# Chunked attention, an MLP and a routed MLP on one core: the first stage in another order, with products of zeros on TensorE

## The chip, the cores and the metric

The kernel runs on one core of a Trainium2 chip. The metric is the device time of one launch in microseconds (us). The kernel before takes 530.31 us, the median of three runs (529.72 to 530.44).

## The reference

Three layers follow one another. Sizes: 4 batches, 8 heads, 768 positions, head width 32, state 16, so 3072 tokens of 256 numbers.

```
# 1: chunked linear attention, chunks of 32
cum = cumsum(log(clip(a)))                  # decay inside a chunk
y   = ((C B^T) * exp(cum_i - cum_j) * causal) x  +  (C state) * exp(cum_i)
state = exp(sum la) * state + sum_j B_j x_j exp(cum_end - cum_j)
# 2: gated MLP, 256 -> 1536 -> 256
x = (silu(x w_gate) * (x w_val)) w_out
# 3: routed MLP, 8 experts, the best one per token
h = relu(x w1[e]);  out = gate * (h w2[e])
```

## The kernel before

The work of layer 1 is cut into 24 *units* of 128 tokens; four units are a *block* of 512 tokens, the width of one product of layer 2. The first block has to be through layer 1 before the first product of layer 2 (line L441, tiles `pg` and `pv`) can start. This opening part, which `first_block` writes out by hand, is called the first stage here. Instructions of an engine run in the order in which the code issues them; an engine that waits holds up all that stands behind it. Loads go through one queue on SyncE (SP), also in order.

A unit u passes these steps, each a function:
- `load` (SP): tiles `xbb` and `cbd`, 128x512 fp32 each (262 kB). There are four buffers of each.
- `weigh` (GpSimd, once VectorE): tile `xw`, L278.
- `scores_mm` (TensorE): 16 products of 64 columns (L291) and 16 of 256 (L297) in two PSUM tiles `pc`. `pc` and one of the two `py` tiles share a ring of three buffers.
- `scores_m` and `states` (VectorE, some of it ScalarE): `mt` (L305) and the states `sv`, `se`, `st`.
- `values_mm` (TensorE, L343 and L353): tiles `py`.
- `values_out`: four VectorE products `y`, `z` (L369 to L372), then a ScalarE cast into `xt` (L374), the high part of the token block.
- `values_low` (VectorE, L380): the low part of `xt`.

The decay factors come once for every two blocks: `setup_ln`, `setup_decay` (`pw`, `W`) and `setup_cum` (`pe`, `er`); `cum_split` leaves `er` and `eh`. `emit_d(b)` makes a tile `du` (L259, GpSimd) out of `er` for block b, and `emit_u(b)` two products `pu` (L270) with copies `U` on ScalarE. `U` of block 0 is needed by `values_out` of units 0 to 3, `U` of block 1 by units 4 to 7.

The MLP weights lie packed in memory. `load_w(f)` brings column tile f of twelve (`wraw`, 786 kB, three buffers). `decode(f, part)` unpacks it: part 0 (ScalarE, `ha`, L403), part "t" (ScalarE, `wv`, L406), parts "b" and "c" (VectorE, `wv`, L412 and L416), part 2 (ScalarE, high half `wh`, L419) and part 3 (low half `wl`, L421, VectorE, or GpSimd for f = 0). The three buffers make `load_w(f + 3)` wait for part "c" of f.

`keep_busy(n)` issues n products that nobody reads (`pi`, L204). After the first stage a loop over i issues per step twelve products of layer 2 (`mlp1_mm`: six `pg`, six `pv`), a silu on ScalarE (`h`, L448), a product on VectorE (`h`, L449), and from i = 2 on six products `py` (L469), with one attention unit in most steps. `pg`, `pv` and the second `py` tile share a ring of three PSUM buffers: the second `pv` waits until L449 has read the first.

Of the kernel before, what the change touches and what calls it, by code (L numbers as in the profile page):

```python
# [9 lines left out]
F32 = mybir.dt.float32  # L10
F32R = mybir.dt.float32r
BF16 = mybir.dt.bfloat16
# [17 lines left out]
BLK = 512  # L30
# [87 lines left out]
def kernel(  # L118
# [5 lines left out]
    nc = tc.nc  # L124
# [64 lines left out]
    def setup_cum(b0, n):  # L189

        p = ps_g("pe", (128, n, 132))
        for b in range(n):
            nc.tensor.matmul(out=p[:, b], lhsT=at[:, 2 * (b0 + b):2 * (b0 + b) + 2].rearrange("k b t c -> k (b t c)"),
                             rhs=c1[:, C_S:C_S + 132], start=True, stop=True)
        nc.scalar.activation(out=er[:, b0:b0 + n], in_=p, func=AF.Exp, scale=-1.0)

    idle_t = []

    def keep_busy(n):

        if not idle_t:
            idle_t.append(ps.tile([128, 2, 256], F32, tag="y0", bufs=1, name="pi"))
        for _ in range(n):
            nc.tensor.matmul(out=idle_t[0], lhsT=r32[:, 0],  # L204
                             rhs=r32.rearrange("p g j -> p (g j)").unsqueeze(1).to_broadcast([128, 2, 256]),
                             start=True, stop=True)

    def silu_first():

        t = ap_.tile([128, 1], F32, name="sf")  # L210
        nc.scalar.activation(out=t, in_=c1[:, C_ME:C_ME + 1], func=AF.Silu)

    def setup_ones():
        p8 = c1[:, C_P8:C_P8 + 8].unsqueeze(2)
        nc.vector.tensor_copy(out=r16.rearrange("p (h n) -> p h n", h=8), in_=p8.to_broadcast([128, 8, 16]))
        nc.vector.tensor_copy(out=r32.rearrange("p g (h i) -> p (g h) i", h=4), in_=p8.to_broadcast([128, 8, 32]))
# [19 lines left out]
    def cum_ends(b0, n, d2):  # L236
        p = ps_g("pe2", (128, 8 * n, 4))
        nc.tensor.matmul(out=p.rearrange("p a b -> p (a b)"), lhsT=r16, rhs=d2.rearrange("p a b c -> p (a b c)"),
                         start=True, stop=True)
        return p  # L240
# [8 lines left out]
    def emit_d(b):  # L249
        if b == 1:  # L250
            d = keep.tile([128, 4, 128], F32R, name="du", tag="yT", bufs=1)
        else:
            d = ap_.tile([128, 4, 128], F32R, name="du", tag="mt", bufs=2)
        o = C_MU + 4 * (b % 2)
        if b == 2:
            for q in range(4):
                nc.scalar.activation(out=d[:, q], in_=er[:, b // 2, 0:128], func=AF.Copy, scale=c1[:, o + q:o + q + 1])
        else:
            nc.gpsimd.tensor_tensor(  # L259
                out=d, in0=er[:, b // 2, 0:128].unsqueeze(1).to_broadcast([128, 4, 128]),  # L260
                in1=c1[:, o:o + 4].unsqueeze(2).to_broadcast([128, 4, 128]), op=ALU.mult)
        return d
# [10 lines left out]
    def weigh(u, e):  # L273

        r = raw[u]
        b, o = divmod(u, 4)
        r["xw"] = ap_.tile([128, 8, 32], F32, name="xw", tag="xw", bufs=3)
        e.tensor_tensor(out=r["xw"], in0=r["x"], in1=W[:, b, o * 8:o * 8 + 8].unsqueeze(2).to_broadcast([128, 8, 32]),  # L278
                        op=ALU.mult)
# [107 lines left out]
    def load_w(f, e=nc.sync):  # L387
        if f >= NF:
            return
        wr[f] = keep.tile([128, 768, 2], I32, name="wraw", tag="raw", bufs=3)  # L390
        e.dma_start(out=wr[f], in_=I["mw"][f].bitcast(I32).rearrange("p (n t) -> p n t", t=2))
# [415 lines left out]
    def first_block():  # L807

        setup_loads()
        load(0)  # L810
        load(1)
        nc.sync.dma_start(out=at0[:, 2:], in_=I["at"][:, 2:])
        load(2)
        load_w(0)
        load(3)
        load_w(1)
        setup_ln(0, 2)
        setup_decay(0, 2)
        setup_cum(0, 1)
        weigh(0, nc.vector)  # L820
        scores_mm(0)
        cum_split(0, 1)
        setup_ones()
        weigh(1, nc.gpsimd)
        d = emit_d(0)
        p = cum_ends(0, 1, cum_ends_d(0, 1))
        scores_m(0)
        cum_store(0, 1, p)
        states(0)
        emit_u(0, d)  # L830
        cum_pairs(1, 8)
        setup_ln(2, NBLK)
        decode(0, 0)
        d = emit_d(1)
        weigh(2, nc.gpsimd)
        for u in range(4):
            scores_mm(u + 1)
            values_mm(u)
            if u == 1:
                setup_decay(2, NBLK)  # L840
                setup_cum(1, 2)
            if u < 3:
                scores_m(u + 1)
                states(u + 1)
            if u in (0, 2):
                decode(u // 2, "t")
            values_out(u)
            if u == 0:
                emit_u(1, d)
                decode(0, "b")  # L850
            if u == 1:
                decode(0, "c")
            if u == 2:
                decode(1, "b")
            keep_busy((0, 4, 4, 6)[u])
            values_low(u)
            load(u + 4)
            if u == 0:
                weigh(3, nc.gpsimd)
            if u == 1:  # L860
                load_w(2)
                load_w(3)
                nc.sync.dma_start(out=c2, in_=I["cst"][:, C1:C_END])
                weigh(4, nc.gpsimd)
                decode(0, 2)
                decode(0, 3, low=nc.gpsimd)
                decode(1, 0)
            if u == 2:
                decode(1, "c")
                silu_first()  # L870
                decode(1, 2)
                weigh(5, nc.gpsimd)
        scores_m(4)
        states(4)
        decode(1, 3)
        decode(2, 0, "t")
        load_w(4)

        todo = {0: 2, 1: 3, 2: 4, 4: 5, 6: 6, 8: 7, 10: 8, 12: 9, 14: 10, 15: 11}
        units = {0: 4, 1: 5, 3: 6, 5: 7, 13: 8, 16: 9, 19: 10, 22: 11}  # L880
        for i in range(2 * NF):
            q, f = divmod(i, HALF)
            b, f = q % 2, f + HALF * (q // 2)
            u = units.get(i)
            w = todo.get(i, NF)
            if i + 1 in units and units[i + 1] > 4:
                weigh(units[i + 1] + 1, nc.vector if i < 16 else nc.gpsimd)
            if u == 7:
                mlp1_down(*late.pop(0))
                scores_mm(u + 1)  # L890
                values_mm(u)
                values_out(u)
                values_low(u)
            p = mlp1_mm(b, 0, BLK, f)
            if u is not None and u != 7:
                scores_mm(u + 1)
                values_mm(u)
            if len(late) == LAG or u == 7:
                mlp1_down(*late.pop(0))
            late.append((b, 0, BLK, f))  # L900
            decode(w, 1)
            h = mlp1_h(p, BLK)
            if w < NF:
                load_w(w + 3)
                decode(w + 1, 0, "t")
            decode(w, 2)
            if u is not None and u != 7:
                values_out(u)
            decode(w, 3)
            if i in (20, 21):  # L910
                turn_y(0, 2 * i - 40)
                turn_y(0, 2 * i - 39)
            if i == 23:
                route_b(0)
            mlp1_split(h, b, 0, BLK, f)
            if i in (7, 13):
                take_part(0 if i == 7 else 1)
            if i == 19:
                take_y(0)
            if u is not None:  # L920
                if u != 7:
                    values_low(u)
                    scores_m(u + 1)
                    states(u + 1)
                load(u + 4)
            if i == 6:
                scores_m(8)
                cum_split(1, 2)
            if i == 7:
                dd.append(cum_ends_d(1, 2))  # L930
            if i == 8:
                cum_store(1, 2, cum_ends(1, 2, dd.pop()))
                cum_pairs(8, NU)
                states(8)
            if i == 9:
                dd.append(emit_d(2))
            if i == 10:
                emit_u(2, dd.pop())
            if 16 <= i < 20:
                setup_route(i - 16)  # L940
            if i == 22:
                route_a(0)
            if i == 21:
                dd.append(emit_d(3))
            if i == 23:
                emit_u(3, dd.pop())
# [190 lines left out]
```

## Time and profile before

| | us |
|---|---|
| median of three runs | 530.31 |
| profiled execution | 530.17 |
| its span | 528.4 |
| around the span | 1.77 |
| TensorE busy | 505.0 (96% of the span) |
| VectorE busy | 289.1 (55%) |
| first product of layer 2 begins at | 24.40 |

The span is what the profiler sees between the first and the last instruction. A time in the trace counts from the span's start. A row of the timeline gives start, duration, engine, line, operation, output and inputs, count, and in brackets the idle time of the engine before it and who ended it.

### The profile page before, as it was taken

How to read it: one execution, taken by the hardware profiler on the slowest of the kernel's cores; microseconds unless marked ns; L12 is line 12 of the kernel's file. 1: busy time of each engine (PE TensorE's matmuls, PEld its weight loads, DVE VectorE, ACT ScalarE, POOL GpSimd, SP SyncE). 2: the span in 40 equal slices, each digit the busy share in tenths (PEclk: the TensorE clock that was granted, in tenths of full speed). 3: DMA queues.
4: the chain of work that ended last, by engine and by line, in shares of the span. 5: the costliest groups of instructions: out<-in, count | busy, mean ns of one | idle time of the engine just before them, and what ended most of it. 6: DMA issues, size and time to landing. Idle time of an engine off the chain costs nothing.

```text
span 528.4 us, 11243 instructions
## 1 busy us (share of the span) xinstructions
PE 505.0 (96%) x4580; PEld 416.7 (79%) x4580; DVE 289.1 (55%) x631; ACT 219.5 (42%) x403; POOL 105.8 (20%) x127
## 2 busy tenths in 40 slices
PE   6889999999999999999999999999999999999990
PEld 3677787778788778888788778888899989999880
DVE  4998786944554544445444554455466564646320
ACT  4785575434333334233333332434454353534220
POOL 3200000220220130005000224211055426240220
PEclk9999999999999999999999999999999999999995
DMA  8954422011230312012100104234188544521100
GB/s 299 338 183 137 155 80 82 25 49 41 82 32 30 103 15 66 3 47 74 21 2 2 43 1 158 84 121 41 41 105 176 162 130 137 153 104 42 40 22 22
DMA packets 20694, 45.55 MB, mean 86 GB/s; under 512 B 4768, under 2 KB 8352, under 8 KB 20640
## 3 DMA queue, kind: packets, MB, share of 16 engines
q1 hardware_dynamic: 17424, 38.29, 26.2%
q0 software_dynamic: 3072, 6.41, 4.1%
q8 instruction: 37, 0.61, 0.6%
q14 instruction: 17, 0.14, 0.1%
q10 hardware_dynamic: 144, 0.11, 0.1%
HBM read 38.30 MB, written 6.50 MB: 85 GB/s over the span
## 4 chain that ended last, share of the span: by engine, by line
PE 76%; issue 11%; DVE 4%; POOL 3%; ACT 2%; DMA 1%; SPq 0%; POOLq 0%; DVEq 0%; ACTq 0%
PE py L469 19%; PE pg L441 18%; PE pv L441 18%; PE ph L758 7%; PE po L779 6%; PE pt L553 2%; POOL out L793 2%; PE pc L297 2%; PE py L353 1%; PE py L343 1%; PE pc L291 1%; DMA xbb<-in_xbb 1%; PE pu L270 1%; DVE wv L412 1%; PE px L747 1%
## 5 line engine op out<-in xcount | busy, mean ns | idle before, releaser
L441 PE MATMUL pg<-xt,wh 128*128 128x512 f32 x288 | 93.2, 404 | 0.3 <-ACT xt L374 0.2
L441 PE MATMUL pv<-xt,wh 128*128 128x512 f32 x288 | 90.4, 395 | 0.0
L449 DVE TENSOR_TENSOR h<-h,pv 128x512 f32<-128x512 f32 x72 | 49.4, 686 | 66.7 <-PE pv L441 55.6
L456 DVE TENSOR_TENSOR hl<-h,hh 128x512 fp32r<-128x512 f32 x72 | 50.2, 697 | 61.7 <-ACT hh L455 61.5
L758 PE MATMUL ph<-xt,hl 128*128 128x512 f32 x288 | 72.7, 394 | 0.0
L779 PE MATMUL po<-hl,hh 128*128 128x256 f32 x384 | 70.1, 283 | 0.0
L441 PEld LDWEIGHTS pv<-xt,wh 128*128 128x128 f32 x288 | 54.2, 188 | 12.8
L779 PEld LDWEIGHTS po<-hl,hh 128*128 128x128 f32 x384 | 60.3, 188 | 2.1
L455 ACT CAST hh<-h 128x512 fp32r<-128x512 f32 x72 | 44.6, 620 | 40.4 <-DVE h L449 40.4
L441 PEld LDWEIGHTS pg<-xt,wh 128*128 128x128 f32 x288 | 52.1, 188 | 11.6 <-ACT xt L374 0.6
L448 ACT ACTIVATE h<-pg 128x512 f32<-128x512 f32 x72 | 42.7, 593 | 41.7 <-PE pg L441 41.7
L614 POOL DMA_INDIRECT slots<-ids,si x24 | 26.0, 1081 | 168.4 <-DVE si L606 163.6
L758 PEld LDWEIGHTS ph<-xt,hl 128*128 128x128 f32 x288 | 51.7, 188 | 9.2
L469 PE MATMUL py<-hh,wh 128*128 128x512 f32 x144 | 58.7, 407 | 0.0
L441 PE MATMUL pg<-xt,wl 128*128 128x512 f32 x144 | 57.0, 396 | 0.3 <-DVE wl L421 0.3
L469 PE MATMUL py<-hl,wh 128*128 128x512 f32 x144 | 56.9, 395 | 0.0
L469 PE MATMUL py<-hh,wl 128*128 128x512 f32 x144 | 56.8, 394 | 0.0
L441 PE MATMUL pv<-xt,wl 128*128 128x512 f32 x144 | 56.8, 394 | 0.0
L779 PE MATMUL po<-hl,hl 128*128 128x256 f32 x192 | 53.9, 281 | 0.2 <-DVE hl L767 0.2
L767 DVE SCALAR_TENSOR_TENSOR hl<-ph,hh 128x512 fp32r<-128x512 f32 x48 | 33.0, 688 | 31.8 <-ACT hh L766 30.8
L766 ACT ACTIVATE hh<-ph 128x512 fp32r<-128x512 f32 x48 | 28.8, 600 | 41.4 <-PE ph L758 24.3
L779 PEld LDWEIGHTS po<-hl,hl 128*128 128x128 f32 x192 | 36.1, 188 | 0.4 <-DVE hl L767 0.4
(140 smaller groups left out, 669.6 us busy)
## 6 DMA issues: line engine op xcount, KB each, us to landing
eraw<-in_ew SPq DMA_DIRECT2D x24, 512.0 KB
wraw<-in_mw SPq DMA_DIRECT2D x12, 768.0 KB
xbb<-in_xbb SPq DMA_DIRECT2D x24, 256.0 KB
cbd<-in_cbd SPq DMA_DIRECT2D x24, 256.0 KB
yd<-yr SPq DMA_DIRECT2D x6, 528.0 KB
slots<-ids,si POOLq DMA_INDIRECT x24
xg<-yd,idx POOLq DMA_INDIRECT x24
out<-ob,idx POOLq DMA_INDIRECT x24
```

What stands on the lines that cost most here:

```text
L297: nc.tensor.matmul(out=r["pc"][g][32 * q:32 * q + 32, 0:256], lhsT=r["bt"][k, 32 * q:32 * q + 32], rhs=r["c"][k, q // 2].rearrange("p h i ...
L441: nc.tensor.matmul(out=t, lhsT=w[:, f, o:o + 128], rhs=xt[:, xp, k, cs], start=n == 0, stop=n == 5)
L448: nc.scalar.activation(out=h, in_=p[0], func=AF.Silu)
L449: nc.vector.tensor_tensor(out=h, in0=h, in1=p[1], op=ALU.mult)
L455: nc.scalar.copy(out=hh, in_=h)
L456: e.tensor_tensor(out=hl, in0=h, in1=hh.bitcast(F32), op=ALU.subtract)
L469: nc.tensor.matmul(out=yb[b][d][:, c:c + m], lhsT=w[:, f, o:o + 128], rhs=h, start=first and n == 0, stop=last and n == 2, skip_group_chec ...
L614: i = nc.gpsimd.indirect_dma_start(out=slots[0:E * upto], out_offset=bass.IndirectOffsetOnAxis(ap=si[:, s:s + 1], axis=0), in_=ids[g][:, o ...
L758: nc.tensor.matmul(out=p, lhsT=self.hl[:, w, o:o + 128], rhs=self.xt[:, xp, k], start=n == 0, stop=n == 5)
L766: nc.scalar.activation(out=hh, in_=p, func=AF.Relu)
L767: nc.vector.scalar_tensor_tensor(out=hl, in0=p, scalar=0.0, in1=hh.bitcast(F32), op0=ALU.max, op1=ALU.subtract)
L779: nc.tensor.matmul(out=self.po[s // 2][:, s % 2], lhsT=h[:, q], rhs=self.hl[:, w, o:o + DM], start=f == 0 and n == 0 and s % 2 == 0, stop= ...
```

## The change

The line numbers of the changed kernel are 12 to 15 higher behind its new function (L259 becomes L271, for example).

- `emit_d(0)` comes ahead of `weigh(1)`.
- A bf16 tile of zeros `zb` is set on VectorE, and nine products of 512 columns with it go to TensorE: five ahead of `setup_decay`, two ahead of `scores_mm(0)`, two behind `cum_ends`.
- `load_w(1)` moves behind `load(4)`, `load_w(2)` behind `load(6)`, `load_w(3)` behind `load(7)`.
- The decode of weight tile 0 moves one to two units later. That of tile 1 moves so that its parts "b", "c" and 2 stand behind unit 3's `values_low`.
- `emit_u(1)` moves from unit 0 to unit 2, `silu_first` (with its table load) from unit 2 to unit 3.
- `weigh(4)` and `weigh(5)` come ahead of the low half of tile 0 on GpSimd.
- `keep_busy` has 2, 2, 4, 4 products in place of 0, 4, 4, 6.

```diff
+    def warm_up(n):
+        if not warm_t:
+            warm_t.append(ap_.tile([128, BLK], BF16, name="zb"))
+            nc.vector.memset(warm_t[0], 0.0)
...
+            nc.tensor.matmul(out=idle_t[0].rearrange("p g j -> p (g j)"), lhsT=warm_t[0][:, 0:128], rhs=warm_t[0],
+                             start=True, stop=True)
...
-        load_w(1)
+        warm_up(5)
         setup_ln(0, 2)
         setup_decay(0, 2)
         setup_cum(0, 1)
+        warm_up(2)
         weigh(0, nc.vector)
         scores_mm(0)
         cum_split(0, 1)
         setup_ones()
+        d = emit_d(0)
         weigh(1, nc.gpsimd)
-        d = emit_d(0)
         p = cum_ends(0, 1, cum_ends_d(0, 1))
+        warm_up(2)
         scores_m(0)
...
-            if u in (0, 2):
-                decode(u // 2, "t")
+            if u == 2:
+                decode(1, 0)
             values_out(u)
...
+            if u == 3:
+                decode(1, "t")
+                silu_first()
...
         scores_m(4)
         states(4)
-        decode(1, 3)
+        decode(1, 1, 2, 3)
         decode(2, 0, "t")
         load_w(4)
```

GpSimd, from its first product on; `xw` is a unit's weighed input and `du` feeds `pu`. Before:

```order
L278 TENSOR_TENSOR xw<-xbb,W 128x256
L259 TENSOR_TENSOR du<-er,c_69 128x512 x2
L278 TENSOR_TENSOR xw<-xbb,W 128x256 x3
L421 TENSOR_TENSOR wl<-wv,wh 128x768
L278 TENSOR_TENSOR xw<-xbb,W 128x256
```

Now:

```order
L271 TENSOR_TENSOR du<-er,c_69 128x512
L290 TENSOR_TENSOR xw<-xbb,W 128x256
L271 TENSOR_TENSOR du<-er,c_69 128x512
L290 TENSOR_TENSOR xw<-xbb,W 128x256 x4
L433 TENSOR_TENSOR wl<-wv,wh 128x768
```

The first `du` no longer stands behind an `xw`, and the low half `wl` of weight tile 0 stands behind all five `xw`.

VectorE, at the end of the first stage: `mt`, `sv`, `se` are unit 4's, the `y`, `z` and `xt` rows unit 3's, and `wv` a weight tile in decode. Before, the `wv` rows are tile 1's, and so is `wl`:

```order
L412 SCALAR_TENSOR_TENSOR wv<-ha,wv 128x768
L380 TENSOR_TENSOR xt<-y_422,xt 128x2x128
L416 SCALAR_TENSOR_TENSOR wv<-wraw,wv 128x768
L369 TENSOR_TENSOR y_497<-py,U 128x192
L370 TENSOR_TENSOR z_498<-py,U 128x128
L371 TENSOR_TENSOR y_497<-py,U 128x64
L372 TENSOR_TENSOR y_497<-y_497,z_498 128x128
L380 TENSOR_TENSOR xt<-y_497,xt 128x2x128
L305 TENSOR_TENSOR mt<-pc,c_69 128x256 x2
L321 SCALAR_TENSOR_TENSOR sv<-se,eb,pc 128x64
L324 SCALAR_TENSOR_TENSOR se<-sv,eb,pc 128x64
L421 TENSOR_TENSOR wl<-wv,wh 128x768
```

Now (the first pair of `wv` is tile 1's, the second tile 2's):

```order
L384 TENSOR_TENSOR y_498<-y_498,z_499 128x128
L392 TENSOR_TENSOR xt<-y_498,xt 128x2x128
L317 TENSOR_TENSOR mt<-pc,c_69 128x256 x2
L333 SCALAR_TENSOR_TENSOR sv<-se,eb,pc 128x64
L336 SCALAR_TENSOR_TENSOR se<-sv,eb,pc 128x64
L424 SCALAR_TENSOR_TENSOR wv<-ha,wv 128x768
L428 SCALAR_TENSOR_TENSOR wv<-wraw,wv 128x768
L433 TENSOR_TENSOR wl<-wv,wh 128x768
L290 TENSOR_TENSOR xw<-xbb,W 128x256
L424 SCALAR_TENSOR_TENSOR wv<-ha,wv 128x768
L428 SCALAR_TENSOR_TENSOR wv<-wraw,wv 128x768
L461 TENSOR_TENSOR h<-h,pv 128x512
```

Tile 1's two `wv` steps have moved from ahead of unit 3's `xt` to behind unit 4's states, directly ahead of the `wl` that needs them.

ScalarE, from unit 3's cast into `xt` to the first silu `h`; `ha` and `wv` are the first steps of a decode, `wh` is its high half. Before:

```order
L419 CAST wh<-wv 128x768
L374 CAST xt<-y_497 128x2x128
L326 ACTIVATE st<-se,eb 128x64
L327 ACTIVATE st<-sv,eb 128x64
L403 ACTIVATE ha<-wraw 128x768
L406 ACTIVATE wv<-wraw 128x768
L448 ACTIVATE h<-pg 128x512
```

Now:

```order
L386 CAST xt<-y_498 128x2x128
L418 ACTIVATE wv<-wraw 128x768
L223 ACT_TABLE_LOAD
L223 ACTIVATE sf<-c_69 128x1
L338 ACTIVATE st<-se,eb 128x64
L339 ACTIVATE st<-sv,eb 128x64
L431 CAST wh<-wv 128x768
L415 ACTIVATE ha<-wraw 128x768
L418 ACTIVATE wv<-wraw 128x768
L460 ACTIVATE h<-pg 128x512
```

Tile 1's `wv`, the table load and tile 1's `wh` now stand between unit 3's cast and the first silu; the `ha` and second `wv` behind them are tile 2's, as before.

## Rows read from the trace of the kernel before

**Rows 1.** Windows: start and end, length, busy us by engine, PEclk, DMA share, GB/s

```profile
10.91:24.80 13.89, 11.93 (x351) 8.29 (x336) 12.28 (x37) 11.07 (x23) 3.70 (x4) 1.00 0.96 343
29.55:33.76 4.21, 2.76 (x13) 1.83 (x11) 4.08 (x12) 2.13 (x5) 0.00 (x0) 1.00 0.70 233
36.00:42.00 6.00, 6.00 (x28) 4.85 (x26) 5.88 (x15) 4.11 (x7) 0.00 (x0) 1.00 0.60 218
```

**Rows 2.** Timeline of TensorE: start, duration, instruction, idle time before it

```profile
3.41 0.69 PE L186 MATMUL pw<-at,c 128*128 128x64 f32 x2 [3.41 <-ACT at L182]
5.24 1.11 PE L297 MATMUL pc<-cbd,xbb 64*32 64x256 f32 x16
8.27 1.22 PE L270 MATMUL pu<-du,r 128*128 128x512 f32 x2 [1.60 <-POOL du L259]
15.90 0.27 PE L186 MATMUL pw<-at,c 128*128 128x128 f32 x1 [0.85 <-issue]
17.60 0.64 PE L297 MATMUL pc<-cbd,xbb 64*32 64x256 f32 x16
24.40 0.96 PE L441 MATMUL pg<-xt,wh 128*128 128x512 f32 x2 [0.21 <-ACT xt L374]
33.76 0.28 PE L291 MATMUL pc<-xw,xbb 64*32 64x64 f32 x7 [1.45 <-DVE mt L305]
```

**Rows 3.** Timeline of VectorE, from the split of the decay on

```profile
5.32 0.30 DVE L226 TENSOR_TENSOR er<-er,eh 128x132 f32<-128x132 f32 x1
7.64 0.22 DVE L316 TENSOR_TENSOR se<-st,pc 128x64 f32<-128x64 f32 x1
10.91 0.76 DVE L305 TENSOR_TENSOR mt<-pc,c 128x256 f32<-128x256 f32 x2 [2.46 <-PE pc L297]
13.47 0.96 DVE L412 SCALAR_TENSOR_TENSOR wv<-ha,wv 128x768 int32<-128x768 int32 x1 [0.65 <-ACT wv L406]
17.85 0.42 DVE L380 TENSOR_TENSOR xt<-y,xt 128x256 fp32r<-128x256 f32 x1 [0.25 <-ACT xt L374]
20.70 1.22 DVE L412 SCALAR_TENSOR_TENSOR wv<-ha,wv 128x768 int32<-128x768 int32 x1
22.17 0.94 DVE L416 SCALAR_TENSOR_TENSOR wv<-wraw,wv 128x768 int32<-128x768 int32 x1
24.38 0.42 DVE L380 TENSOR_TENSOR xt<-y,xt 128x256 fp32r<-128x256 f32 x1 [0.47 <-ACT xt L374]
25.89 0.95 DVE L421 TENSOR_TENSOR wl<-wv,wh 128x768 fp32r<-128x768 f32 x1
27.68 0.96 DVE L412 SCALAR_TENSOR_TENSOR wv<-ha,wv 128x768 int32<-128x768 int32 x1 [0.50 <-ACT wv L406]
29.55 0.68 DVE L449 TENSOR_TENSOR h<-h,pv 128x512 f32<-128x512 f32 x1
32.96 0.75 DVE L305 TENSOR_TENSOR mt<-pc,c 128x256 f32<-128x256 f32 x2
```

**Rows 4.** Timeline of GpSimd in the first stage

```profile
6.61 0.61 POOL L278 TENSOR_TENSOR xw<-xbb,W 128x256 f32<-128x256 f32 x1 [6.17 <-DMA xbb<-in_xbb]
7.18 2.17 POOL L259 TENSOR_TENSOR du<-er,c 128x512 fp32r<-128x512 f32 x2
12.01 0.62 POOL L278 TENSOR_TENSOR xw<-xbb,W 128x256 f32<-128x256 f32 x1 [2.09 <-DMA xbb<-in_xbb]
18.62 1.85 POOL L421 TENSOR_TENSOR wl<-wv,wh 128x768 fp32r<-128x768 f32 x1 [2.75 <-ACT wh L419]
```

**Rows 5.** Timeline of ScalarE: the first table load, a high half, two steps of a decode

```profile
1.16 1.28 ACT L176 ACT_TABLE_LOAD   x1 [1.16 <-PEq L1127]
23.15 0.83 ACT L419 CAST wh<-wv 128x768 fp32r<-128x768 f32 x1 [0.57 <-DVE wv L416]
25.95 0.90 ACT L403 ACTIVATE ha<-wraw 128x768 f32<-128x768 f32 x1
26.75 0.90 ACT L406 ACTIVATE wv<-wraw 128x768 int32<-128x768 uint32 x1
```

More of the change, by code (lines that the diff above doesn't have):

```diff
@@ L205, in keep_busy @@
                              rhs=r32.rearrange("p g j -> p (g j)").unsqueeze(1).to_broadcast([128, 2, 256]),
+                             start=True, stop=True)
+    warm_t = []
+    def warm_up(n):
+        if not warm_t:
+            warm_t.append(ap_.tile([128, BLK], BF16, name="zb"))
+            nc.vector.memset(warm_t[0], 0.0)
+            idle_t.append(ps.tile([128, 2, 256], F32, tag="y0", bufs=1, name="pi"))
+        for _ in range(n):
+            nc.tensor.matmul(out=idle_t[0].rearrange("p g j -> p (g j)"), lhsT=warm_t[0][:, 0:128], rhs=warm_t[0],
                              start=True, stop=True)
@@ L832, in first_block @@
         setup_ln(2, NBLK)
-        decode(0, 0)
         d = emit_d(1)
@@ L837, in first_block @@
             scores_mm(u + 1)
+            if u == 2:
+                emit_u(1, d)
             values_mm(u)
@@ L844, in first_block @@
                 states(u + 1)
-            if u in (0, 2):
-                decode(u // 2, "t")
+            if u == 2:
+                decode(1, 0)
             values_out(u)
             if u == 0:
-                emit_u(1, d)
+                decode(0, 0, "t")
+            if u == 1:
                 decode(0, "b")
-            if u == 1:
+            if u == 2:
                 decode(0, "c")
-            if u == 2:
-                decode(1, "b")
-            keep_busy((0, 4, 4, 6)[u])
+            if u == 3:
+                decode(1, "t")
+                silu_first()
+            keep_busy((2, 2, 4, 4)[u])
             values_low(u)
@@ L858, in first_block @@
             if u == 0:
+                load_w(1)
                 weigh(3, nc.gpsimd)
             if u == 1:
+                weigh(4, nc.gpsimd)
+            if u == 2:
                 load_w(2)
+                weigh(5, nc.gpsimd)
+                decode(0, 2)
+                decode(0, 3, low=nc.gpsimd)
+            if u == 3:
                 load_w(3)
                 nc.sync.dma_start(out=c2, in_=I["cst"][:, C1:C_END])
[L864 to L872, printed above, removed]
         scores_m(4)
         states(4)
-        decode(1, 3)
+        decode(1, 1, 2, 3)
         decode(2, 0, "t")
```

## The prediction

> **What bounds the kernel now.** I read the table of windows first, then the timeline engine by engine. Over the whole run TensorE is the bound, so the reader should look for the place from which it stays full. From 36 us on it is busy for 6.00 us of 6.00 [rows 1]. Its last long wait ends at 33.76: 1.45 us, released by VectorE's `mt` of unit 5, which ran at 32.96 [rows 2, 3]. So the end of the run moves as that `mt` moves, and later work behind it keeps its order.
>
> What sets that `mt` is VectorE. From 10.91, where `mt` of unit 1 starts, to 24.80, where unit 3's low part ends (24.38 and 0.42), VectorE is busy for 12.28 of 13.89 us; from the first `h` at 29.55 to 33.76 for 4.08 of 4.21 us [rows 1, 3]. TensorE's first product of layer 2 at 24.40 waits for the cast of unit 3 [rows 2], itself a link of this chain. Ahead of 10.91 VectorE had waited 2.46 us for unit 1's scores [rows 3]. These stood behind `pu`, which began at 8.27 after 1.60 us idle and waited for `du` on GpSimd [rows 2]; and `du` stood behind an `xw` that started at 6.61 because its input landed then [rows 4], though `er`, which `du` reads, was ready at 5.62 (5.32 and 0.30) [rows 3].
>
> [...]
>
> **The change, part by part.** I follow the VectorE chain: where it starts, how long it is, and what it hands to TensorE.
>
> *Start of the chain.* With `du` first on GpSimd it can run from 5.65 and, at 2.17/2 = 1.08 us [rows 4], be done at 6.75 in place of 8.27. Two other things then come late. One is the nine products of zeros. A `pu` takes 1.22/2 = 0.61 us at the lower level [rows 2], my upper bound; 0.35 us, that by the ratio 0.64/1.11, is the lower one; for the first ones I take 0.48, the middle. Nothing shows when the first could start; I take 1.2, about where ScalarE begins [rows 5]. Five then end at 1.2 + 2.4 = 3.6 (2.95 to 4.25), against 3.41 where `pw` started, so all that hangs on the decay comes 0.2 us late (0 to 0.85). The other four fill gaps: TensorE idled 1.60 us ahead of `pu`. The other late comer is a PSUM buffer: unit 1's scores need one that unit 0's `se` still reads, until 7.86 (7.64 and 0.22) [rows 3].
>
> The forecast takes it that the clock is at the upper level by then, since TensorE now has work from about 1.2 on with hardly a gap, where before it had its first long work at 8.27. Then `pu` is over before unit 0's states are, and unit 1's scores start at about 7.86 + 0.2 = 8.1. They take 0.64 us and a head of some 0.2 for the 64-column products: `mt` of unit 1 starts at 9.0, 1.9 us sooner.
>
> [...]
>
> *Length of the chain.* From 10.91 to the first `h` at 29.55 it was 18.64 us. Nothing is taken out of it: tile 1's two `wv` steps (20.70, 22.17) only move behind unit 3's low part and unit 4's states. What changes is the waits and one stretched instruction [rows 3, 5]:
> - The wait of 0.65 us ahead of tile 0's first `wv` (13.47) goes, since that step now comes one unit later. Unit 0's low part then has nothing between it and its cast, and waits as unit 3's does: 0.47. Together -0.18.
> - Tile 0's ScalarE steps now stand ahead of unit 1's cast, and they, with `W` and `er`, can hold its low part: 0 to 0.55, I take 0.30 in place of the 0.25 at 17.85: +0.05.
> - The 1.22 us of the `wv` at 20.70 should be like the 0.96 at 27.68: -0.26. This is a single stretched row; if it stretches again the term is nothing.
> - Tile 1's `wl` now stands directly behind its `wv`, with ScalarE's `wh` between: VectorE waits 0.83 + 0.05 = +0.88.
> - The old wait of 0.50 at 27.68 goes. In its place VectorE's next `wv` (tile 2) waits for ScalarE, which begins `ha` and `wv` only behind that `wh`: 26.75 - 25.95 + 0.90 = 1.70 us, against VectorE's own `wl` and `xw`, 27.68 - 25.89 - 0.50 = 1.29. So +0.41 - 0.50 = -0.09.
>
> Sum 18.64 - 0.18 + 0.05 - 0.26 + 0.88 - 0.09 = 19.04 us. The first `h` starts at 9.0 + 19.04 = 28.04, against 29.55: 1.51 us sooner. Unit 3's low part itself then ends at 28.04 less the stretch from it to `h`: 29.55 - 24.80 = 4.75, and 0.88 - 0.09, and the two `wv` at 29.55 - 27.68 = 1.87. That is 20.63, 4.17 sooner, of which 2.66 is given back ahead of `h`.
>
> *What that is worth.* From `h` to unit 5's `mt` the order of VectorE is as before, so TensorE's wait ends at 33.76 - 1.51 = 32.25 and the rest follows.
>
> *What is hidden.* The first product of layer 2 needs tile 0's `wl`, which GpSimd (1.85 us [rows 4]) now makes late in the stage. It may end about 1 us behind unit 3's cast, and delay the first twelve products by that. But TensorE then waits for ScalarE anyway: the second `pg` needs no PSUM buffer until the first is read by a silu that stands behind tile 2's steps, and the second `pv` waits for `h`. The first products move by about 4.1 us and `h` by 1.5, so this is worth nothing up to about 2.6 us, and beyond it each us costs one. The table load (1.28 [rows 5]) now lies after the last cast; ScalarE has that time, since its next due piece is `wh` behind the two `wv`. The 2 fewer `keep_busy` products stand in TensorE's idle time either way.
>
> *The loads.* They are in order and the DMA engines are full, 0.96 of the time at 343 GB/s [rows 1]. Unit 3's `xbb` lands at 12.01 [rows 4], with nothing changed ahead of it. Behind it come `cbd` 3, both tiles of unit 4, and only then weight tile 1: 3 x 0.262 + 0.786 = 1.57 MB, 4.6 us, so 16.6. Its first use on ScalarE, ahead of unit 2's cast, comes at about 17. This is close: 0.4 us of cover, and behind it each us costs VectorE one.
>
> *Sum.* 530.17 - 1.51 = 528.66 by the profiled execution, which is 0.14 below the median of the runs; so 528.8.
>
> **The rivals.**
> 1. *The clock rises later*, with the first `pu` or unit 1. For it: nothing in the trace shows TensorE on zeros, and before, its work from 3.41 on left it slow through the `pu` at 8.27. Against it: the far earlier start of the work. Then the four other zeros cost 4 x 0.48 less the 1.60 of idle time, and the 0.2 from the five: `pu` at 8.27 + 0.5 = 8.8; faster `pu` and scores give back 0.6 and 0.5, so `mt` starts near 10.6 - 0.4 = 10.2 to 10.6. `h` at 29.2 to 29.6: 530.0 to 530.4, no change.
> 2. *The clock rises as before, at 15.90, and the zeros only stand in the way.* This is the other side. At 0.61 us, five make the decay 0.85 late and four add 2.44, less 1.60 + 0.2 of gaps: `pu` 1.5 us later, at 9.8, `mt` at 12.4, `h` at 12.4 + 19.04 = 31.4, 1.9 us late: 532.2. It decides from where `pu` begins later than 8.8. For it: both levels stand in the rows. Against it: as above.
> 3. *The weights come too late*: tile 1 lands behind 17, and ScalarE, waiting for it ahead of unit 2's cast, holds VectorE. If the loads slip by 2 us, 528.8 + (2 - 0.4) = 530.4. For it: the DMA engines are full. Against it: the order ahead of tile 1 only gets lighter, and SyncE issues each of these loads sooner than it lands.
> 4. *More is gained*: no wait at unit 1's low part (-0.3) and tile 2's steps not late (-0.4), with `mt` at 8.6 (-0.4): 527.7.
>
> **How the numbers follow.** Forecast 0.52 (its own range 527.9 to 529.6); rival 1 0.18; rival 2 0.10; rival 3 0.08; rival 4 0.12. 0.2% is 1.06 us, about what can be told from no change. Faster: 0.80 of the forecast (its gain of 1.5 has an error of nearly 1), all of rival 4, a tenth each of 1 and 3: 0.42 + 0.12 + 0.03 = 0.57, and I say 0.58. Slower: most of rival 2, a tenth of the others: 0.15. Same: 0.27. The range reaches from rival 4's bound at 527.3 to 530.8, where rival 2 and a part of 1 and 3 stay outside.
>
> **What would show it.** `pu` at 8.0 or sooner, unit 0's sixteen L297 products or at least unit 1's at about 0.64 us; `mt` of unit 1 at 9.0; unit 3's low part ending near 20.6 with the first product of layer 2 just ahead; a wait of VectorE for `wh` of 0.9 there and one for tile 2's `wv`; `h` at 28.0 and TensorE's last long wait ending near 32.3, with dense work behind it. It is wrong if unit 1's L297 products still take 1.1 us, if ScalarE's second `ha` waits for DMA, or if a new wait of TensorE stands behind 34.

## The result: slower by 0.66%, and the profile after

The changed kernel took 534.08 us (median of 4 runs, 532.09 to 534.97), the kernel before 530.38 beside it (529.72 to 530.64): a ratio of 1.0066, 95% interval 1.004 to 1.0091. Forecast were 528.8 us, with a range of 527.3 to 530.8. The profiled execution took 532.09 us, the shortest of the four (span 529.9, before 528.4), so its trace explains +1.5 us of the 1.92 between the two profiled executions (530.17 before); the other 0.4 lies around the span, 2.19 us against 1.77. A profile near the median follows with the experiment after_again.

VectorE in the changed kernel, columns as in [rows 3]:

```profile
5.94 1.03 DVE L243 TENSOR_TENSOR d<-er,c 128x32 fp32r<-128x32 f32 x1
9.11 0.76 DVE L317 TENSOR_TENSOR mt<-pc,c 128x256 f32<-128x256 f32 x2 [0.37 <-PE pc L309]
14.40 0.36 DVE L381 TENSOR_TENSOR y<-py,U 128x192 f32<-128x192 f32 x1 [1.30 <-PE py L365]
18.56 0.28 DVE L384 TENSOR_TENSOR y<-y,z 128x128 f32<-128x128 f32 x1
20.39 0.36 DVE L381 TENSOR_TENSOR y<-py,U 128x192 f32<-128x192 f32 x1 [0.34 <-PE py L365]
21.00 1.63 DVE L384 TENSOR_TENSOR y<-y,z 128x128 f32<-128x128 f32 x1
23.09 0.43 DVE L392 TENSOR_TENSOR xt<-y,xt 128x256 fp32r<-128x256 f32 x1 [0.47 <-ACT xt L386]
27.45 0.96 DVE L433 TENSOR_TENSOR wl<-wv,wh 128x768 fp32r<-128x768 f32 x1 [0.90 <-ACT wh L431]
29.11 0.96 DVE L424 SCALAR_TENSOR_TENSOR wv<-ha,wv 128x768 int32<-128x768 int32 x1 [0.37 <-ACT wv L418]
30.98 0.68 DVE L461 TENSOR_TENSOR h<-h,pv 128x512 f32<-128x512 f32 x1
34.40 0.75 DVE L317 TENSOR_TENSOR mt<-pc,c 128x256 f32<-128x256 f32 x2
```

The chain starts 1.80 us sooner than before (10.91, [rows 3]). Unit 3's low part ends at 23.09 + 0.43 = 23.52, only 1.28 sooner (24.80), and the first `h` starts at 30.98, 1.43 later (29.55). Two large rows between are new: a wait of 1.30 for `py`, and a `y` that took 1.63 us where the same form takes 0.28.

TensorE, columns as in [rows 2]:

```profile
1.18 2.31 PE L217 MATMUL pi<-zb 128*128 128x512 bf16 x5 [1.18 <-DVE zb L214]
7.41 0.81 PE L282 MATMUL pu<-du,r 128*128 128x512 f32 x2
8.34 0.63 PE L309 MATMUL pc<-cbd,xbb 64*32 64x256 f32 x14
10.66 0.63 PE L309 MATMUL pc<-cbd,xbb 64*32 64x256 f32 x14
11.47 0.43 PE L365 MATMUL py<-cbd,st 64*32 64x64 f32 x22
14.04 0.31 PE L365 MATMUL py<-cbd,st 64*32 64x64 f32 x7 [2.15 <-issue]
23.11 1.25 PE L453 MATMUL pg<-xt,wh 128*128 128x512 f32 x2 [1.62 <-ACT xt L386]
35.20 0.28 PE L303 MATMUL pc<-xw,xbb 64*32 64x64 f32 x7 [1.59 <-DVE mt L317]
```

The scores at 8.34 are unit 1's, those at 10.66 unit 2's. The wait for `py` comes from here: in the middle of unit 1's 32 L365 products TensorE stops for 2.15 us, and no engine or semaphore is named ("issue"). Its last long wait ends at 35.20, 1.44 later than before [rows 2], and behind that nothing differs: the span less the end of this wait is 494.6 us before, 494.7 after, and 494.5 to 494.9 in all the experiments. So that one number stands for the span below.

GpSimd, columns as in [rows 4]:

```profile
5.77 1.15 POOL L271 TENSOR_TENSOR du<-er,c 128x512 fp32r<-128x512 f32 x1 [5.34 <-DVE er L238]
20.66 1.82 POOL L433 TENSOR_TENSOR wl<-wv,wh 128x768 fp32r<-128x768 f32 x1 [2.37 <-ACT wh L431]
```

The `du` is out at 6.92. The `wl` ends at 22.48; VectorE's `y` of 1.63 began during it and ended at 22.63.

What the DMA engines did around TensorE's stop (the window of 11.5 to 14.1 us; queue, packets, MB, share of 16 engines), and the instruction queue over the whole run, from the page:

```profile
q1 hardware_dynamic: 356, 1.02, 102.1%
q8 instruction: 1, 0.02, 2.2%
...
q8 instruction: 37, 0.61, 0.6%
```

Instructions too come by DMA, 0.61 MB in 37 packets: some 16 kB each. One falls into this window, in which the data loads alone fill the engines (102.1%).

### The profile page after: what moved, and what is told of

It is laid out like the page before. It is cut to its first block, busy times and chain, and to the rows that moved or that the text cites. A ratio compares the mean times of both kernels' runs of the same rounds, so it can differ in the third digit from the quotient of the medians.

```text
span 529.9 us, 11255 instructions
## 1 busy us (share of the span) xinstructions
PE 507.4 (96%) x4587; PEld 417.1 (79%) x4587; DVE 292.0 (55%) x632; ACT 219.9 (41%) x403; POOL 105.7 (20%) x127
## 4 chain that ended last, share of the span: by engine, by line
PE 77%; issue 11%; DVE 5%; POOL 2%; ACT 2%; DMA 0%; SPq 0%; POOLq 0%; ACTq 0%
PE py L481 19%; PE pg L453 18%; PE pv L453 18%; PE ph L770 7%; PE po L791 6%; PE pt L565 2%; POOL out L805 2%; PE pc L309 2%; PE py L365 1%; PE py L355 1%; PE pc L303 1%; DVE wv L424 1%; PE px L759 1%; POOL xg L729 1%; PE pu L282 1%
```

## The experiments

All are timed against the kernel before on the same chip. "Start" is unit 1's `mt`, "low" the end of unit 3's low part, `h` the first one, "end" the end of TensorE's last long wait, all in us of one profiled execution; the stop is that "issue" of TensorE which is the longest (when it ends).

| kernel | start | stop (ends) | low | h | end | median us (n) | ratio, 95% |
|---|---|---|---|---|---|---|---|
| before | 10.91 | 0.91 (21.25) | 24.80 | 29.55 | 33.76 | 530.38 | |
| after | 9.11 | 2.15 (14.04) | 23.52 | 30.98 | 35.20 | 534.08 (4) | 1.0066 [1.004, 1.0091] |
| after_again | 9.10 | 2.97 (14.85) | 25.71 | 33.12 | 37.34 | 533.94 (5) | 1.0057 [1.0043, 1.0071] |
| no_zeros | 9.90 | 0.26 (19.29) | 23.29 | 30.69 | 34.90 | 531.93 (12) | 1.0035 [1.0019, 1.0051] |
| du_zeros | 9.07 | 1.67 (14.70) | 25.17 | 29.91 | 34.12 | 530.64 (12) | 1.0007 [0.9998, 1.0015] |
| du_only | 9.94 | 2.96 (22.95) | 26.48 | 31.22 | 35.44 | 530.52 (11) | 0.9998 [0.9989, 1.0007] |
| wl_vec | 9.12 | 1.88 (13.79) | 23.32 | 31.57 | 35.78 | 532.5 (5) | 1.0037 [1.0025, 1.005] |
| keep9 | 9.19 | 2.11 (14.08) | 24.96 | 32.36 | 36.58 | 533.01 (6) | 1.0051 [1.0033, 1.0069] |
| short_zeros | 9.20 | 2.57 (14.29) | 25.44 | 32.90 | 37.12 | 533.57 (4) | 1.0056 [1.0041, 1.0071] |
| w0_late | 9.09 | 1.98 (19.17) | 23.17 | 31.43 | 35.65 | 532.1 (7) | 1.0032 [1.0021, 1.0043] |
| no_zeros_v | 10.12 | 0.88 (19.64) | 22.81 | 31.06 | 35.27 | 532.0 (7) | 1.003 [1.0019, 1.0042] |
| light | 9.14 | 2.95 (19.92) | 25.36 | 32.02 | 36.24 | 532.42 (7) | 1.0034 [1.0023, 1.0046] |
| light_nz | 9.93 | 1.64 (19.34) | 24.32 | 31.11 | 35.34 | 532.4 (5) | 1.0046 [1.0032, 1.006] |
| before_plus | 11.26 | 1.38 (16.23) | 25.65 | 29.22 | 33.57 | 530.12 (11) | 1.0001 [0.999, 1.0012] |

The profile of after is the shortest of its runs, that of du_only (531.83) the longest of its eleven.

The stops stand at fixed counts. Count TensorE's products from the start, zeros and `keep_busy` included: nine of the profiles have a first stop, with 218 or 219 products ahead of it, and nine have a second one, with 343 ahead, whatever these products are. So 125 products and as many weight loads lie between, 250 instructions (before: from the `pw` at 15.90, [rows 2], to the scores products at 21.25). Over the whole run of after TensorE's 4587 products and as many loads are 248 for each of the 37 packets of q8. And each of these eighteen stops ends 2.2 to 2.7 us after a q8 packet has begun, as narrow windows of the DMA view show: at 13.40 in before (the stop ends at 15.90), 11.64 in after (14.04), 12.42 in after_again (14.85). So TensorE waits there for its next instructions, as far as counts and times can tell.

**no_zeros: the change without the nine products of zeros.**

```diff
-warm_up(5)
...
-warm_up(2)
...
-warm_up(2)
```

> The changed kernel without its nine products of zeros. Theory A: what the zeros gain is swallowed by TensorE's stall inside unit 1's values (2.15 us, 11.89 to 14.04, put down to issue), because the stall ends when a block of instructions has come in by DMA. By it unit 1's mt starts later (10 to 11 in place of 9.11), TensorE still stalls within some 18 instructions of the same place, the stall ends at 14 to 15.5, and the profiled execution takes 532 to 533. Rival: the zeros carry their gain through: the time is 1.5 us or more above that of the changed kernel.

TensorE in no_zeros:

```profile
7.29 1.20 PE L282 MATMUL pu<-du,r 128*128 128x512 f32 x2
8.63 1.10 PE L309 MATMUL pc<-cbd,xbb 64*32 64x256 f32 x16
```

`pu` and unit 1's scores run at the lower level here (that of the 1.11 us at 5.24 [rows 2]; the upper is that of the 0.64 at 17.60, and the granted clock reads 1.00 in both stretches), and the start is 0.79 us later than in after; yet the median is 2 us lower (the two intervals overlap a little). The zeros do buy the early start, but it doesn't last to the low part, which ends sooner here (23.29): no stop stands in unit 1's values, and the only one is short and comes later. A stop near the old place, ending at 14 to 15.5, and 532 to 533 us were expected; both were missed. What is slower than before, 0.35%, lies behind the low part: this comes 1.51 us sooner than in before, but from there to `h` it takes 7.40 us in place of 4.75.

**du_zeros and du_only: the kernel before, with the first `du` ahead, with and without the zeros.**

```diff
+d = emit_d(0)
 weigh(1, nc.gpsimd)
...
+warm_up(5), +warm_up(2), +warm_up(2)   (du_zeros alone)
```

> The kernel before with two parts of the change alone: the first du ahead of the xw on GpSimd, and the nine products of zeros. Loads, decode and keep_busy as before. Unit 1's mt starts near 9.1 as in the changed kernel. Theory A with B: TensorE's stall for instructions comes sooner and is longer than the 0.85 us of before, and ends near 14 to 15; GpSimd's wl of tile 0 lies earlier and holds nothing of the last unit; so a part of the 1.8 us comes through: 529 to 530. Rival: the later weights and decode carried the loss or gain of the change alone: then this one is 528.5 (all of the earlier start kept) or 532 and more (the start itself is what costs).

> The kernel before with the first du ahead of the xw on GpSimd, and nothing else. Theory A: unit 1's mt starts near 9.9, as without zeros; TensorE comes to the end of its instructions about 1 us sooner than before (15.05), and the next block is there at about 14 to 15, so the stall is small or as before (0 to 0.85), the clock doesn't fall, and of the 1 us between nothing and 0.8 comes through: 529.7 to 530.5. Rival: the start was worth its whole 1 us or more: 529.4 or less.

Both take the time of before; for du_zeros 529 to 530 was expected, and missed. Its early start is gone already at VectorE's first step of weight tile 0, and the cause is the load of that tile. VectorE and ScalarE in du_zeros:

```profile
13.47 0.96 DVE L424 SCALAR_TENSOR_TENSOR wv<-ha,wv 128x768 int32<-128x768 int32 x1 [2.49 <-ACT wv L418]
11.29 0.89 ACT L415 ACTIVATE ha<-wraw 128x768 f32<-128x768 f32 x1 [1.76 <-DMA wraw<-in_mw]
```

This VectorE step starts at 13.47 in before too [rows 3], and at 13.44 in du_only: ScalarE gets tile 0 at 11.2 to 11.3 in all three, and VectorE's wait grows from 0.65 to 2.49 and 1.58, by as much as the start is earlier (1.84 and 0.97). The stop comes on top. TensorE in du_zeros:

```profile
14.70 0.32 PE L365 MATMUL py<-cbd,st 64*32 64x64 f32 x8 [1.67 <-issue]
```

Behind it VectorE waits 1.05 us for unit 3's scores, and the low part ends 0.37 later than in before. So neither the earlier `du` nor the zeros are worth anything while tile 0's decode stands where it stood, and the stop doesn't need the late decode. From low to `h` it is 4.74 us in both, as before (4.75).

**short_zeros: each product of zeros cut into four of 128 columns,** 27 more pairs of weight load and product, hardly more time (the last eight take 0.62 us, the two in after 0.61). If TensorE runs out of instructions, the stop must come 27 pairs sooner.

```diff
+for k in range(4):
+    s = slice(k * 128, k * 128 + 128)
+    matmul(out=idle[:, s], lhsT=warm[:, 0:128], rhs=warm[:, s])
```

> The changed kernel with each product of zeros of 512 columns cut into four of 128, so the same columns but 54 more TensorE instructions ahead of everything else. Theory A (TensorE runs out of instructions; the next block comes by DMA and is there at about 14 whatever TensorE does): the stall put down to issue stands 54 instructions earlier in the program, at the end of unit 1's L355 products or the first of L365 (27 pairs of weight load and product sooner), begins near 11.4 and still ends at 13.8 to 14.7. Rival (the stall belongs to that product: its operand, its PSUM tile or a wait that the profile doesn't show): it stays behind the same number of L365 products, with 7 of 32 left.

TensorE's rows (L357 and L367 are L355 and L365 of after):

```profile
11.12 0.61 PE L357 MATMUL py<-mt,xw 64*32 64x64 f32 x30
14.29 0.24 PE L357 MATMUL py<-mt,xw 64*32 64x64 f32 x1 [2.57 <-issue]
14.30 0.28 PE L367 MATMUL py<-cbd,st 64*32 64x64 f32 x7
14.37 0.22 PE L357 MATMUL py<-mt,xw 64*32 64x64 f32 x1
14.38 0.48 PE L367 MATMUL py<-cbd,st 64*32 64x64 f32 x25
```

In after, 32 of unit 1's first kind and 25 of its second ran ahead of the stop; here 30 and none: 2 + 25 = 27 pairs sooner. As expected, the stop sits at a count of TensorE's instructions, not at a datum, and it ends 0.25 us from where it ended in after although TensorE got there sooner.

**w0_late: wl_vec (below), and the load of weight tile 0 behind those of unit 4,** 0.79 MB less ahead of the stop.

```diff
-load_w(0)
 load(3)
...
 load(4)
+load_w(0)
...  (its first ScalarE and VectorE steps one unit later)
```

> The kernel wl_vec with the load of weight tile 0 behind unit 4's loads, and its decode a unit later: 0.786 MB less ahead of the units' data in the queue. Theory A with the loads as the cause: the block of instructions waits behind the loads, about 2 us of which (0.786 MB at 343 GB/s) are now behind it, so TensorE's stall ends at 12 to 12.5 in place of 13.8, or is gone, the clock stays at the upper level from 14 to 17, and unit 3's low part ends 1 us or more sooner than wl_vec's 23.3. Rival: the block takes as long whatever the loads do: the stall ends at 13.8 to 14.7 as in wl_vec.

TensorE, and the window in which it stops next (columns as in [rows 1]):

```profile
11.45 0.88 PE L365 MATMUL py<-cbd,st 64*32 64x64 f32 x29
12.27 0.49 PE L186 MATMUL pw<-at,c 128*128 128x128 f32 x2
19.17 0.33 PE L303 MATMUL pc<-xw,xbb 64*32 64x64 f32 x5 [1.98 <-issue]
```

```profile
16.00:20.00 4.00, 2.02 (x36) 1.35 (x43) 2.48 (x7) 3.40 (x7) 0.69 (x1) 0.90 1.03 379
```

The first stop is gone: the q8 packet begins at 9.39, in wl_vec at 11.12, although unit 1's `mt` starts within 0.03 us in both. `mt` of unit 3 comes at 14.77 where after has 16.80, and then the next block is late by 1.98 us, in the stretch in which the shifted load now fills the DMA engines. Both weight tiles' loads now stand together: tile 0 is used from 16.60 on, after ScalarE had waited 2.20 us for it, and VectorE waits 1.49 for that decode. The low part, expected 1 us or more sooner than wl_vec's 23.32, comes at 23.17.

**wl_vec: tile 0's `wl` on VectorE, behind unit 3's low part,** so that nothing runs on GpSimd beside the `y`.

```diff
-decode(0, 3, low=nc.gpsimd)    (u == 2)
+decode(0, 3)                   (u == 3)
```

> The changed kernel with the low half of weight tile 0 on VectorE, directly behind unit 3's low part, in place of GpSimd. Theory B: unit 3's last y (1.63 us in the changed kernel, 0.28 elsewhere) was held until GpSimd's 1.82 us wl ended. By it this y takes 0.28, unit 3's cast starts about 1.35 sooner (near 21.3), VectorE has 0.95 of work more behind it, and the first h comes about 0.4 sooner (30.6). Rival: the 1.63 has another cause (instructions coming in late, or the DMA): it stays above 1 us and h comes 0.95 later.

VectorE's rows:

```profile
22.14 0.28 DVE L384 TENSOR_TENSOR y<-y,z 128x128 f32<-128x128 f32 x1
22.90 0.42 DVE L392 TENSOR_TENSOR xt<-y,xt 128x256 fp32r<-128x256 f32 x1 [0.47 <-ACT xt L386]
23.24 0.95 DVE L433 TENSOR_TENSOR wl<-wv,wh 128x768 fp32r<-128x768 f32 x1
```

The `y` is back to 0.28: the 1.35 us were GpSimd's. But `h` did not come at the expected 30.6: from low to `h` it is now 8.25 us instead of 7.46, as the `wl` stands in that stretch, and low itself came hardly sooner: in this execution the clock fell after the stop (granted 0.70 as a mean over 12 to 16 us), unit 3's sixteen scores products took 0.72, and `xt` of unit 1 ran at 17.05 instead of 16.45.

**no_zeros_v: no_zeros, tile 0's `wl` on VectorE, unit 5's `xw` one unit later.**

```diff
 (no_zeros)
-decode(0, 3, low=nc.gpsimd)
+decode(0, 3), weigh(5, nc.gpsimd)   (u == 3)
```

> The kernel no_zeros with the low half of weight tile 0 on VectorE behind unit 3's low part, and the weighing of unit 5 on GpSimd moved there too, so that GpSimd runs nothing beside the last two units' y and low parts. Theory B: unit 2's low part (0.83 us in no_zeros) goes back to 0.42 and unit 3's last y (1.6) to 0.28; with 0.95 more work on VectorE the first h comes 0.6 to 0.8 sooner than 30.69, and the time is 530.9 to 531.5. Rival: the collisions were covered: 531.9 or more.

Again 0.28 for the `y`, and no better time: the 0.85 us that the collision had cost in no_zeros (its `y` took 1.13) meet a stop that has grown from 0.26 to 0.88, with VectorE waiting 1.46 for `py`. The time is the rival's (531.9 or more).

**keep9: nine `keep_busy` products in unit 3 in place of four,** to hold the clock over TensorE's gap there.

```diff
-keep_busy((2, 2, 4, 4)[u])
+keep_busy((2, 2, 4, 9)[u])
```

> The changed kernel with nine keep_busy products in unit 3 in place of four. Theory C: the 1.62 us idle ahead of the first product of layer 2 let the clock fall to the lower level (products at 0.63 us, a granted clock of 0.75 from 24 to 30), and the timed runs that lie up to 2.9 us above the profiled one fell lower or for longer. By it the first twelve products run at 0.40, the window 24 to 30 reads 1.00, the median falls from 534.1 to about 532 and the spread of the runs from 2.9 to under 1 us. Rival: the fall costs nothing, as TensorE has 2.6 us to spare there: the median stays within 0.7 of 534.

Windows of keep9, columns as in [rows 1]:

```profile
12.00:16.00 4.00, 1.92 (x14) 1.75 (x15) 2.58 (x10) 1.43 (x3) 1.23 (x2) 0.76 0.89 324
16.00:20.00 4.00, 4.00 (x104) 2.32 (x104) 2.59 (x10) 2.78 (x9) 0.62 (x1) 0.82 0.35 125
```

The runs still lie 3.2 us apart (532.02 to 535.2). The clock is 1.00 behind the gap that was filled (24 to 30 us; after: 0.75) and here falls already from the stop on. So that gap isn't the only place where it is lost, and my theory that filling it would settle the spread fell. The median, 533.01, lies between the two forecasts (532, and within 0.7 of 534).

**light and light_nz: the weight loads spread, one tile at a time, `wl` on VectorE between unit 3's `y` and low part; with and without zeros.**

```diff
 load(4)
+load_w(0)
...
 load(6)
+load_w(1)
...
-decode(0, 3, low=nc.gpsimd)
+decode(0, 3)     (between values_out(3) and values_low(3))
...  (and the other moves that the text below names)
```

> The changed kernel (zeros and first du kept) with its weight loads spread out, one tile at a time: tile 0 behind unit 4's loads, tile 1 behind unit 6's, tile 2 behind unit 7's, then tile 3; tile 0 decoded two units later, its low half on VectorE between unit 3's y and its low part; tile 1's first steps right ahead of unit 3's y; unit 6's weighing in VectorE's wait for tile 1's high half, and tile 2's ha ahead of that high half on ScalarE. Theory A (blocks of instructions wait behind the loads): with at most some 1.3 MB ahead of a block neither stall of about 2 us is there; unit 3's low part ends near 21, VectorE takes 6.7 us from there to h (7.46 in the changed kernel), h starts at 27.7 to 28.5, and the time is 528.6 to 529.5. Rival: the stalls come whatever the loads do, then h comes at 30 or later and the time is 531 or more.

> The kernel light without its nine products of zeros. Theory A: TensorE is slower at first and comes to the end of its first instructions at about 14, by when the block is there; unit 1's mt starts near 10, and what the zeros win in light (about 0.9 us at mt) is what separates the two: 529.3 to 530.3. Rival: the zeros make no difference, as VectorE or the loads bind: the two lie within 0.3.

TensorE in light:

```profile
19.92 0.26 PE L303 MATMUL pc<-xw,xbb 64*32 64x64 f32 x5 [2.95 <-issue]
```

light has no first stop, and its second, 2.95 us, is among the longest. The loads are the same bytes in another order, and the DMA share is 0.91 from 16 to 20 us. The weights come late as well: ScalarE waits 2.39 us for tile 0, and VectorE 1.66 for its decode. Expected were 528.6 to 529.5 for it: missed. With this order the zeros make no difference.

**after_again: the changed kernel once more,** since its first profile was its shortest run.

> The changed kernel once more, for a second profile and more runs, since its first profiled run was the fastest of four (532.09, median 534.08). Theory C: TensorE's stall of about 2 us in unit 1's values lets its clock fall, either in 14 to 18 us (then unit 1's low part and the later ones come 1 us or more later, and the run takes 533 to 535) or only later (then 532). Median 533 to 534.5. Rival: the first profile is typical and the spread has its cause behind 36 us: TensorE's last long wait then ends at 35.2 again in a run of 533 or more.

VectorE's waits at unit 1's values and low part, TensorE, then the windows:

```profile
15.33 0.36 DVE L381 TENSOR_TENSOR y<-py,U 128x192 f32<-128x192 f32 x1 [2.24 <-PE py L365]
18.11 0.42 DVE L392 TENSOR_TENSOR xt<-y,xt 128x256 fp32r<-128x256 f32 x1 [1.03 <-ACT xt L386]
14.85 0.43 PE L365 MATMUL py<-cbd,st 64*32 64x64 f32 x7 [2.97 <-issue]
17.89 0.78 PE L309 MATMUL pc<-cbd,xbb 64*32 64x256 f32 x16
37.34 0.28 PE L303 MATMUL pc<-xw,xbb 64*32 64x64 f32 x7 [0.75 <-DVE mt L317]
```

```profile
12.00:16.00 4.00, 1.15 (x10) 0.98 (x11) 1.72 (x8) 1.50 (x2) 1.16 (x2) 0.85 0.91 353
16.00:20.00 4.00, 4.00 (x105) 2.45 (x103) 2.69 (x8) 2.29 (x7) 0.12 (x2) 0.72 0.48 150
```

This execution (534.15) is near the median: its end, 37.34, comes 3.58 later than before, and 0.4 more lies around the span (2.15 against 1.77); the medians differ by 3.7. The stop is 0.82 longer than in after's first profile, and TensorE comes out of it with the clock falling (0.72 as a mean over 16 to 20 us, 1.00 in the first profile). Unit 3's scores begin 2.13 us later (17.89 against 15.76), and `h` 2.14 later. That parts in two: from the end of the stop to these scores TensorE runs the same instructions without a wait, in 3.04 us here (14.85 to 17.89) and in 1.72 in after (14.04 to 15.76). So 0.81 is the later end of the stop and 1.32 the lower level.

**before_plus: the kernel before, tile 1's `wl` between unit 3's `y` and low part, tile 2's first steps ahead of unit 4's states,** to see whether a shorter chain behind low helps by itself.

```diff
+decode(1, 3)          (u == 3, ahead of keep_busy)
+decode(2, 0, "t")     (ahead of scores_m(4), states(4))
```

> The kernel before with the stage's start left alone, and two moves at its end: weight tile 1's low half wl between unit 3's y and its low part, where VectorE waited 0.47 us for the cast, and tile 2's first two ScalarE steps ahead of unit 4's states, so that VectorE no longer waits 0.50 us for them. If the chain of VectorE up to unit 5's mt sets the end, as the sum of the span behind TensorE's last long wait says (494.6 us in every run so far), the first h comes at 28.7 in place of 29.55 and the time falls by 0.8: 529.6. If the bound lies elsewhere (TensorE's blocks of instructions, the loads), it stays within 0.3 of the kernel before.

The stretch from unit 1's `mt` to `h` is 17.96 us against 18.64, but it starts 0.35 later, and the end is 33.57, where TensorE had waited only 0.45 for `mt`: its own work is then nearly the bound. The time is that of before (529.6 was expected). No version here beats the kernel before.

## Why the prediction was wrong

**What bounds it** was right: the span moves with the end of TensorE's last long wait, the rest being 494.5 to 494.9 us in fourteen profiles, and that end with VectorE's chain. The time around the span, 0.4 us of the loss, stood in no term.

**Start of the chain**: right. The five zeros took 2.31 us (2.4 assumed), `pu` came at 7.41 with its two products in 0.81, unit 1's scores in 0.63 for fourteen, and `mt` at 9.11 (forecast 9.0). Luck has a part in the 9.11: `se` freed the buffer at 8.31 and not at 7.86, since unit 0's scores, behind two of the zeros, were done at 6.74 (before 6.35), but unit 1's 64-column products, which the sum put behind it, began at 8.16. Rivals 1 and 2, a clock that rises late or as before, are out.

**Length of the chain**: this step failed. From `mt` to the end of the low part the forecast was 20.63 - 9.0 = 11.63 us; it took 23.52 - 9.11 = 14.41, 2.78 more. The waits ahead of unit 0's and unit 1's low part came as forecast (0.47 and 0.30). Two rows give 2.65 of the 2.78; the rest is nearly all a wait of 0.34 for unit 3's `py`, less 0.24 of a `y` that had been stretched before.
- 1.30: VectorE's wait for `py`. The sum had no term for TensorE stopping by itself. The row stood in [rows 2], 0.85 us ahead of 15.90 with "issue" as its cause, and I read it as a mark for the clock only. There the stop lay ahead of a `pw`, for the decay of a later unit, off the chain but for at most the 0.25 us at 17.85 [rows 3]. The zeros put nine pairs of weight load and product into the stream ahead of it (two more `keep_busy` and two fewer `pu` cancel out); it now comes eight pairs sooner in the program, with seven L365 and one `pw` behind it that had been ahead (218 products ahead of it there, 219 here), and so in the middle of unit 1's values, for which VectorE waits. It also grew, to 2.15. Shown from three sides: it moves with the count of instructions (short_zeros), none stands in these values without the zeros (no_zeros), and it goes when 0.79 MB of loads ahead of it go, to come back at the next block (w0_late). It cost 0.85 us before, with a DMA share of 0.77 from the start of the q8 packet to the end of the stop (13.40 to 15.90), and 2.15 in the changed kernel, with 1.05 (11.64 to 14.04); in after_again 2.97, with 0.91 in 12 to 16 us.
- 1.35: the `y` of 1.63, in "What is hidden". I asked what GpSimd's late `wl` does to TensorE, and not to VectorE, which it held. Shown by wl_vec and no_zeros_v, 0.28 each. In after this `y`, whose two inputs lie in SBUF, ended 0.15 us behind the `wl`; the `z` and `y` ahead of it, which read `py` in PSUM, ran beside the same `wl` in 0.28 and 0.21 us (at 20.67 and 20.87), as in unit 2 (at 18.23 and 18.43). The sign stood in the kernel before: its `y` of 0.52 also ended 0.15 us behind a `wl` (18.62 and 1.85, [rows 4]), and the `wv` of 1.22 that the sum took for a single stretched row began during a GpSimd `xw`. The same befell `d` at the new start: 1.03 us in place of 0.18, ending 0.05 behind the `du`; it cost little, as unit 0's scores were done at 6.74 and it at 6.97.

Before, VectorE and GpSimd:

```profile
5.87 0.18 DVE L231 TENSOR_TENSOR d<-er,c 128x32 fp32r<-128x32 f32 x1
20.10 0.52 DVE L372 TENSOR_TENSOR y<-y,z 128x128 f32<-128x128 f32 x1
20.42 0.67 POOL L278 TENSOR_TENSOR xw<-xbb,W 128x256 f32<-128x256 f32 x1
```

**What is given back behind the low part**: right. 7.41 forecast, 30.98 - 23.52 = 7.46 measured, with 0.90 for `wh` and 0.37 for tile 2's `wv`. This is why the sign turned: 2.71 us are handed back for certain, against 4.17 that were to be won ahead of it, of which 1.28 came. From `h` to unit 5's `mt` 3.42 us, before 3.41.

**The loads** (rival 3) bind, as that rival says, but through TensorE's instructions and not through weight tile 1: no ScalarE step of that tile waited for DMA. Where tile 0's decode is early (du_zeros, du_only) or its load late (w0_late, light), they bind through tile 0. I had given it 0.08 and 530.4.

**The clock**: it rises as forecast (unit 1's scores in 0.63 us, 1.10 without the zeros); that it would stay up was assumed without a word. Windows of after and, last, one of wl_vec:

```profile
12.00:16.00 4.00, 1.96 (x43) 1.41 (x47) 2.66 (x9) 2.33 (x6) 1.23 (x2) 1.00 0.92 336
16.00:20.00 4.00, 4.00 (x170) 2.66 (x155) 3.66 (x12) 3.34 (x9) 0.62 (x1) 1.00 0.61 197
24.00:30.00 6.00, 5.75 (x101) 4.39 (x101) 4.66 (x8) 5.26 (x9) 0.00 (x0) 0.75 0.72 248
12.00:16.00 4.00, 2.21 (x14) 2.00 (x15) 2.81 (x9) 1.51 (x4) 1.10 (x2) 0.70 0.83 314
```

In after's first profile it is 1.00 up to 20 us and 0.75 in 24 to 30; after_again has 0.85 and 0.72 from the stop on. With the longer stop that makes the other 2 us of the median: 0.81 by the stop and 1.32 by the lower level, as reckoned with after_again. The stop's length alone doesn't decide: the clock fell behind 1.88 us in wl_vec and 2.11 in keep9, and stayed at 1.00 behind 2.15 in after's first profile.

**Open**: no row names the engine of the q8 packets; that they are TensorE's follows from the counts and the eighteen times alone. Between wl_vec and w0_late only the loads differ ahead of the packet, and it begins 1.73 us sooner with fewer of them; whether it then waits in its queue or is asked for later isn't told apart, nor why it begins up to 1.3 us apart in profiles that reach the stop at the same time (11.12 in wl_vec, 12.42 in after_again). The 0.4 us around the span has no cause shown: it is 2.13 to 2.24 us in every run of after, after_again, keep9 and short_zeros, and 1.75 to 2.13 in the others. A version with the change's order and neither stop was not reached, so whether the 1.5 us would then come through is not shown.

## What to carry to other kernels

Put a price on every idle row of the engine you speed up, those named "issue" too (0.85 us here, then 2.15), and ask where it falls once the order or the number of instructions has changed: off the path it costs nothing, on it all of it. While loads filled the DMA engines (share 0.83 to 1.03 in the 4 us around the stops of 1.6 us and more), TensorE's instructions came late here too, as far as counts and times can tell, and 27 more pairs of filler loads and products moved the place where it ran out of them by 27 pairs (short_zeros). When moving a GpSimd operation, look which VectorE operations with both inputs in SBUF now fall beside it: here a `y` of 0.28 us took 1.63. And before paying for an earlier start, look whether a load further down holds the chain anyway, as that of weight tile 0 does in du_zeros.

## What was not expected of the hardware

- TensorE stops for 0.26 to 2.97 us, mostly inside groups of equal products; the 4 us around the stops of 1.6 us and more read 311 to 379 GB/s. Putting 27 pairs more into the stream moves the stop by exactly 27 pairs, and in the first stage of fourteen profiles it stands only behind 218 or 219 products, or behind 343.
- With nine bf16 products of 512 columns of zeros, the first from 1.18 us on, two `pu` take 0.81 us at 7.41 and 14 of unit 1's scores products 0.63; without them (no_zeros) it is 1.20 at 7.29, and 1.10 for 16.
- A `y` of 0.28 us takes 1.63, 1.56 (keep9), 1.55 (short_zeros) or 1.54 us (after_again) beside GpSimd's `wl` of 1.82 to 1.85.
